# A two-stage kernel on one core: output bursts placed between the next batch's inverse transforms, and four bursts of the first gate kept for a later slot

## The chip, the cores and the metric

The kernel runs on one core of a Trainium2 chip. The metric is the device time of one execution in microseconds. Before the change it is 217.06 us (median of 8 runs, 214.51 to 221.0). The engines named here are TensorE (PE; its weight loads are PEld), VectorE (DVE), ScalarE (ACT), GpSimd (POOL) and SyncE (SP), which only issues DMAs in this kernel.

## What is computed

Attention with eight heads, of which some see all earlier positions and the others only the first four and the last 64; then a gated long convolution over the sequence. For a batch of 4, a sequence of 768, 8 heads of 64, and 512 channels:

```python
scores = scale * np.matmul(q, k.transpose(0, 1, 3, 2))
scores = np.where(mask[None], scores, -1e9)      # causal; and sink or window where not retrieval
a = np.exp(scores - scores.max(-1, keepdims=True))
x = np.matmul(a / a.sum(-1, keepdims=True), v)   # then (batch, seq, 512)

x1, x2, x3 = np.split(x @ w_proj, 3, axis=-1)
X2 = np.fft.rfft(x2, n=S, axis=1)
H = np.fft.rfft(filter_fft, n=S, axis=0)[None]
y = x1 * np.fft.irfft(X2 * H, n=S, axis=1) * x3
out = y @ w_out
```

## The kernel before

**Slots.** The main loop goes over sixteen pairs of heads (n = 0 to 15; four pairs make a batch). One pass, a *slot*, issues for pair n the scores in three thirds of two chunks each (`emit_chunks`, L362, each chunk followed by an exp on ACT into `pT`, L377), a mask multiplication on DVE (`emit_masking`, L384), and for pair n-1 the product with v (`emit_values`, 42 matmuls at L395) and the division (`emit_norm`, L405 and L406). The result `attn` is turned into `xT`, either by PE and a DVE copy (L413, L415) or by a transposing DMA (L417).

**Loads.** Each slot also issues on SP the loads of v (pair n+2) and of q and k (pair n+3), has POOL cast q, k and v to bf16 (L115), and, from pair 6 on, has a transposing DMA make `qkT` for pair n+2 (L147). SP and POOL keep the order in which the kernel's code runs. PE, DVE and ACT keep it until slot 5 (`order.close()` at L595); from there on a scheduler places the instructions when the kernel is built, and every engine then runs its own list in that fixed order.

**Gates.** The second half is a generator, `moe(b, xT)`, here called gate b+1. Whatever it issues between two `yield`s is a *burst*; `gate_step()` in the main loop runs one burst. Slot 4 has three gate steps and every later slot five; a gate that ends hands over to the next. A gate has 21 bursts:

- three that project x2 (eight matmuls at L428, a copy, a sum and a difference, L433 and L434);
- the first projection of x1 (L444, copied at L452), then three forward transforms X (six matmuls at L301, copied at L488), whose nine products with the filter (L479 to L481) are put into a list and taken from it one or two at a time;
- five that alternate between the product g = x1 · x3 (L498, reading the projection of x3 from PSUM) and the next projection of x1;
- three inverse transforms, `convolve(cb, by)`: six matmuls into `c_ps` (L460), a copy of one half on ACT (L463), the sum and the difference on DVE (L465, L466), and the multiplication by g into `y` (L467);
- the fourth channel block in three bursts: projection of x1, `convolve`, and the multiplication by the projected x3 (L510);
- three output bursts: eight matmuls each with `w_out` (L516), a copy to `o_sb` on ACT (L526) and a write of 512 KB from SP (L527).

The fourth gate runs after the attention has ended and has a finer output stage of its own (L531 to L554).

**Buffers.** PSUM is four bank pairs used in turn under one tag (`bank_pair`), by scores, values, turns and gates alike. `y` and `g` have one buffer each, and serve in the set-up under the tags "y" and "g" for `angle`, `size`, `filt` and `fold`. `o_sb` has two.

Of the kernel before, what the change touches and what calls it, by code (L numbers as in the profile page):

```python
# [9 lines left out]
FP32 = mybir.dt.float32  # L10
BF16 = mybir.dt.bfloat16
# [33 lines left out]
def kernel(  # L45
# [13 lines left out]
    nc = tc.nc  # L59

    B, H, S, D = q.shape
    NT = S // 128
    DM = moe_w_proj.shape[0]
    NC = DM // 128
# [4 lines left out]
    HS = S // 2  # L69
    NM = HS // 128  # L70
# [6 lines left out]
    msb = ctx.enter_context(tc.tile_pool(name="moe_sb", bufs=1))  # L77
# [6 lines left out]
    state = {}  # L84
# [18 lines left out]
    BIASED = 4  # L103
# [111 lines left out]
    )  # L215

    turns = msb.tile([128, NM, HS], I32, name="turns", tag="P")
    angle = msb.tile([128, NM, HS], FP32, name="angle", tag="g")
    size = msb.tile([128, NM, HS], FP32, name="size", tag="y")
    for m in range(NM):  # L220
        nc.scalar.activation(out=turns[:, m], in_=fcol, func=AF.Copy, scale=tfrac[:, m:m + 1])
    emit_cast(state[0])
# [73 lines left out]
    def emit_forward(src, tiles, matrix=G):  # L296

        ps = bank_pair("X_ps")
        for u, (t, r) in enumerate(tiles):
            for m in range(NM):  # L300
                nc.tensor.matmul(ps[:, u, :], lhsT=matrix[:, t, m, :], rhs=src[:, r, m, :],  # L301
                                 start=(m == 0), stop=(m == NM - 1))
        return ps
# [4 lines left out]

    def setup_steps():
        filt = state["filt"]  # L310
        fold = msb.tile([128, 2, NM, DM], BF16, name="fold", tag="y")
        nc.vector.tensor_add(fold[:, 0], filt[:, 0:NM, :], filt[:, NM:NT, :])
        nc.vector.tensor_sub(fold[:, 1], filt[:, 0:NM, :], filt[:, NM:NT, :])
        yield

        def put(engine, out, in_, w):
            if engine is nc.scalar:
                engine.activation(out=out, in_=in_, func=AF.Copy, scale=w / S)
            else:
                engine.tensor_scalar(out=out, in0=in_, scalar1=w / S, scalar2=None, op0=ALU.mult)  # L320


        ps = emit_forward(fold, ((0, 0), (1, 0)))
        for out_, in_, w in ((HA[:, 0, 0, :], ps[:, 0], 1), (HA[:, 0, 1, :], ps[:, 0], 0),
                             (HB[:, 0, 0, :], ps[:, 1], 2), (HB[:, 0, 1, :], ps[:, 1], 0)):
            nc.scalar.activation(out=out_, in_=in_, func=AF.Copy, scale=scales[:, w:w + 1])
        put(nc.scalar, HA[0:1, 0, 1, :], ps[0:1, 1], 1.0)
        yield
        ps = emit_forward(fold, ((2, 1), (3, 1)))
        put(nc.vector, HA[:, 1], ps[:, 0, None, :].to_broadcast([128, 2, DM]), 2.0)  # L330
        put(nc.vector, HB[:, 1, 0, :], ps[:, 1], -2.0)
        put(nc.vector, HB[:, 1, 1, :], ps[:, 1], 2.0)
        yield
        put(nc.vector, HA[:, 2], emit_forward(fold, ((4, 0), (5, 1))), 2.0)
        yield
        nc.scalar.activation(out=HB[:, 2], in_=emit_forward(fold, ((6, 0), (7, 1))), func=AF.Copy, scale=scales[:, 3:4])
        yield
# [84 lines left out]
    def moe(b, xT):  # L422
# [11 lines left out]
            nc.vector.tensor_sub(x2[:, 1, m, :], x2s[:, 0], x2s[:, 1])  # L434
            yield
        P = msb.tile([128, 3, 2, DM], BF16, name="P")
        g = msb.tile([128, NC - 1, S], BF16, name="g")
        y = msb.tile([128, NC, S], BF16, name="y")

        def project(part, cb):  # L440
            ps = bank_pair("x13_ps")
            for s in range(2):
                for cc in range(NC):
                    nc.tensor.matmul(ps[:, s, 0:HS],  # L444
                                     lhsT=wproj[:, cc, part * DM + cb * 128:part * DM + (cb + 1) * 128],
                                     rhs=xT[:, cc, s * HS:s * HS + HS],
                                     start=(cc == 0), stop=(cc == NC - 1))
            return ps[:, :, 0:HS]

        def first(cb):  # L450
            x1s = msb2.tile([128, 2, HS], BF16, name="x1s")
            nc.scalar.copy(out=x1s, in_=project(0, cb))  # L452
            return x1s

        def convolve(cb, by):
            ch = slice(cb * 128, (cb + 1) * 128)
            ps = bank_pair("c_ps")
            for r in range(2):
                for n, (tile_no, t, u) in enumerate(((2 * r, r, 0), (2 * r + 1, r, 1), (4 + r, 2, r))):
                    nc.tensor.matmul(ps[:, r, 0:HS], lhsT=P[:, t, u, ch], rhs=Gi[:, tile_no],  # L460
                                     start=(n == 0), stop=(n == 2))
            evs = msb2.tile([128, HS], FP32, name="evs")
            nc.scalar.copy(out=evs, in_=ps[:, 0, 0:HS])  # L463
            conv = msb2.tile([128, S], BF16, name="conv")
            nc.vector.tensor_add(conv[:, 0:HS], evs, ps[:, 1, 0:HS])  # L465
            nc.vector.tensor_sub(conv[:, HS:S], evs, ps[:, 1, 0:HS])  # L466
            nc.vector.tensor_mul(y[:, cb, :], conv, by)  # L467

        products = []

        def multiply(t, X):
            if t == 2:
                swapped = msb.tile([128, 2, DM], BF16, name="swapped")
                nc.sync.dma_start(out=swapped[0:64], in_=X[64:128])
                nc.sync.dma_start(out=swapped[64:128], in_=X[0:64])
            else:
                swapped = X[:, ::-1, :]
            m2 = msb2.tile([128, 2, DM], BF16, name="m2")
            products.append(lambda: nc.vector.tensor_mul(P[:, t], X, HA[:, t]))  # L479
            products.append(lambda: nc.vector.tensor_mul(m2, swapped, HB[:, t]))  # L480
            products.append(lambda: nc.vector.tensor_add(P[:, t], P[:, t], m2))  # L481

        x1s = first(0)
        yield
        for t in range(3):
            X = msb2.tile([128, 2, DM], BF16, name="X", bufs=3)
            ps = emit_forward(x2, ((0, 0), (1, 1)), G2) if t == 2 else emit_forward(x2, ((2 * t, t), (2 * t + 1, t)))
            nc.scalar.copy(out=X, in_=ps)  # L488
            multiply(t, X)
            if t > 0:  # L490
                products.pop(0)()
            yield
        for cb in range(NC - 1):
            if cb > 0:
                x1s = first(cb)
                products.pop(0)()
                yield
            nc.vector.tensor_mul(g[:, cb, :].rearrange("p (s t) -> p s t", s=2), x1s, project(2, cb))  # L498
            for product in range(2 if cb else 1):
                products.pop(0)()  # L500
            yield
        for cb in range(NC - 1):
            convolve(cb, g[:, cb, :])
            yield
        x1s = first(NC - 1)
        yield
        convolve(NC - 1, x1s.rearrange("p s t -> p (s t)"))
        yield
        last_y = y[:, NC - 1, :].rearrange("p (s t) -> p s t", s=2)
        nc.vector.tensor_mul(last_y, last_y, project(2, NC - 1))  # L510
        yield

        def emit_out(ps, i, cbs):
            for cb in cbs:
                for n in range(ps.shape[1]):
                    nc.tensor.matmul(ps[:, n, :], lhsT=y[:, cb, (i + n) * 128:(i + n + 1) * 128],  # L516
                                     rhs=wout[:, cb, :], start=(cb == 0), stop=(cb == NC - 1))
# [18 lines left out]
        for i in range(NT):  # L536
# [15 lines left out]
            else:  # L552
                nc.scalar.copy(out=o_last[:, i], in_=ps[i][:, 0])
            nc.sync.dma_start(out=out[b, i * 128:(i + 1) * 128, :], in_=o_last[:, i])  # L554
        yield


    emit_loads(1)
# [4 lines left out]
    emit_v(state[0])  # L563
    emit_loads(3)

    gates = []

    def gate_step():
        while gates:
            try:  # L570
                next(gates[0])
                return
            except StopIteration:
                gates.pop(0)

    def emit_weights(n):
        if n == 0:
            state["filt"] = filt = msb.tile([128, NT, DM], BF16, name="filt", tag="g")
            nc.gpsimd.dma_start(out=filt, in_=moe_filter_fft.rearrange("(t p) c -> p t c", p=128))
            emit_matrix()  # L580
        for part in {2: (1,), 4: (0, 2)}.get(n, ()):
            cols = slice(part * DM, part * DM + DM)
            nc.gpsimd.dma_start(out=wproj[:, :, cols], in_=moe_w_proj.rearrange("(c p) n -> p c n", p=128)[:, :, cols])
        if n == 7:
            nc.gpsimd.dma_start(out=wout, in_=moe_w_out.rearrange("(c p) n -> p c n", p=128))
# [3 lines left out]
    for n, (b, hp) in enumerate(pairs):  # L589
# [75 lines left out]
            emit_prep(state[n + 2])  # L665
        if hp == 0:
            gates.append(moe(b - 1, last["xT"]))
        gate_step()
        if n <= BY_PE and hp > 0:
            emit_turn(last)  # L670
        emit_chunks(st, 2)
        emit_masking(st, 2)
        if n == 5:
            emit_inverse_matrix()
        gate_step()
    last = state[N - 1]
    emit_values(last)
    emit_norm(last)
# [3 lines left out]
    gates.append(moe(B - 1, xT))  # L682
    while gates:
        gate_step()


# [33 lines left out]
```

## Time and profile before

| what | value |
|---|---|
| median of 8 runs | 217.06 us (214.51 to 221.0) |
| the profiled execution | 214.91 us, its span 213.1 us |
| granted clock of PE, mean over the span | 0.997 |
| DMA moved | 35.27 MB, 166 GB/s over the span |
| scores' exps, L377 (ACT) | 96, 83.2 us |
| projections, L444 (PE) | 256, 45.6 us |
| convolve matmuls, L460 (PE) | 96, 17.7 us |
| output matmuls, L516 (PE) | 92, 21.5 us |
| output copies, L526 (ACT) | 9, 1014 ns each |
| writes of o_sb | 9 of 512 KB, 4.0 us from issue to landing (median) |

The profile is of one execution, and all sums inside it go against 214.91 us. Busy PE is not PE at its peak: matmuls overlap, so what eight of them cost the queue is read from the starts on the timeline (8 of 128x512 in 1.73 to 1.83 us), not from the mean of one.

### The profile page before, as it was taken

The page shows a single profiled execution, that of the slowest core. Times are in us where ns is not written, and L with a number is a line of the kernel's source. Part 1 is how long each engine was busy: PE and PEld are TensorE (multiplying, and loading weights), DVE is VectorE, ACT ScalarE, POOL GpSimd, SP SyncE. Part 2 cuts the span into 40 slices and gives each one's busy share as a digit, 9 for nine tenths or more (in the row PEclk, how much of TensorE's full clock was granted, in tenths as well). Part 3 has the DMA queues.
Part 4 walks back from the last instruction along what each step waited for, and adds up shares of the span by engine and source line. Part 5 has one row for each costly group of instructions (what it writes and reads, how often), then busy time and mean ns, then how long its engine had stood idle before and what let it go on. Part 6 is the DMA issues. An engine that isn't in the chain of part 4 may idle for free.

```text
span 213.1 us, 4337 instructions
## 1 busy us (share of the span) xinstructions
PE 192.2 (90%) x1763; PEld 106.1 (50%) x1763; DVE 153.5 (72%) x254; ACT 147.6 (69%) x183; POOL 68.2 (32%) x110
## 2 busy tenths in 40 slices
PE   7879998898987979989977978999999899999991
PEld 2346766444545554536454535445456464445641
DVE  7847877995799797416798697437796971368970
ACT  7799886996874758568966575797968723772421
POOL 6499366905370164350433351513000000000000
PEclk9999999999999999999999999999999999999998
DMA  5999999998999999969988989992530203402007
GB/s 155 270 305 203 291 268 230 184 213 165 195 200 165 201 230 159 246 249 216 187 177 148 202 136 210 215 264 67 98 78 11 42 0 119 180 0 49 0 36 260
DMA packets 89939, 35.27 MB, mean 166 GB/s; under 512 B 80320, under 2 KB 86464, under 8 KB 89920
## 3 DMA queue, kind: packets, MB, share of 16 engines
q1 hardware_dynamic: 87024, 32.13, 69.3%
q0 software_dynamic: 2896, 2.88, 8.6%
q8 instruction: 13, 0.21, 0.4%
q14 instruction: 6, 0.05, 0.1%
HBM read 24.65 MB, written 6.29 MB: 145 GB/s over the span
## 4 chain that ended last, share of the span: by engine, by line
PE 44%; DVE 28%; DMA 9%; ACT 8%; SPq 3%; issue 3%; POOL 2%; ACTq 0%; DVEq 0%; POOLq 0%
PE x_ps L444 13%; PE x_ps L428 9%; PE out_ps L516 7%; DMA qk_f<-in_k_dram 7%; DVE pT L384 4%; PE att L395 4%; PE X_ps L301 4%; ACT pT L377 4%; DVE m L480 3%; DVE P L479 3%; SPq L95 3%; PE sc L362 3%; PE c_ps L460 3%; DVE conv L465 3%; DVE P L481 3%
## 5 line engine op out<-in xcount | busy, mean ns | idle before, releaser
L377 ACT ACTIVATE pT<-sc 128x1024 bf16<-128x1024 f32 x96 | 83.2, 921 | 18.9 <-PE sc L362 14.4
L444 PE MATMUL x_ps<-xT,wproj 128*128 128x384 bf16 x256 | 45.6, 326 | 5.0 <-DVE conv L466 1.9
L115 POOL CAST qk_bf<-qk_f 128x768 bf16<-128x768 f32 x31 | 27.0, 878 | 68.1 <-DMA qk_f<-in_q_dram 60.0
L384 DVE TENSOR_TENSOR pT<-pT,mask 128x1024 bf16<-128x1024 bf16 x36 | 26.3, 731 | 14.2 <-ACT pT L377 14.1
L444 PEld LDWEIGHTS <-wproj 128*128 128x128 bf16 x256 | 24.2, 98 | 23.3 <-issue 4.8
L362 PE MATMUL sc<-qkT 64*128 64x512 bf16 (+3 forms) x256 | 28.4, 307 | 3.2 <-DVE qkT L143 1.2
L395 PEld LDWEIGHTS <-pT 128*128 128x128 bf16 x672 | 23.2, 97 | 4.2 <-DVE pT L384 1.0
L395 PE MATMUL att<-v_aug,pT 128*128 128x65 bf16 x352 | 24.0, 193 | 1.3 <-DVE pT L384 0.9
L428 PE MATMUL x_ps<-wproj,xT 128*128 128x512 bf16 x96 | 22.4, 379 | 1.3 <-ACT o_sb L526 0.8
L516 PE MATMUL out_ps<-wout,y 128*128 128x512 bf16 x92 | 21.5, 380 | 0.9 <-DVE y L510 0.9
L395 PE MATMUL att<-v_far,pT 128*128 128x65 bf16 x320 | 21.0, 193 | 0.0
L452 ACT CAST x1s<-x_ps 128x768 bf16<-128x768 f32 x16 | 12.9, 806 | 9.7 <-PE x_ps L444 7.1
L362 PEld LDWEIGHTS <-qkT 64*128 64x128 bf16 x256 | 10.0, 94 | 18.8 <-issue 12.4
L460 PE MATMUL c_ps<-Gi,P 128*128 128x384 bf16 x96 | 17.7, 326 | 1.9 <-DVE conv L466 1.1
L347 POOL TENSOR_TENSOR v_far<-v_aug,vmask 128x520 bf16<-128x520 bf16 x16 | 18.5, 1158 | 1.3
L526 ACT COPY o_sb<-out_ps 128x1024 f32<-128x1024 f32 x9 | 9.0, 1014 | 11.7 <-PE out_ps L516 8.9
L301 PE MATMUL X_ps<-x,G 128*128 128x512 bf16 x72 | 16.9, 380 | 0.1
L406 DVE TENSOR_TENSOR attn<-att,rec 128x768 bf16<-128x768 f32 x16 | 15.3, 956 | 0.5
L432 ACT CAST x2s<-x_ps 128x1024 bf16<-128x1024 f32 x12 | 12.4, 1030 | 3.5 <-PE x_ps L428 3.2
L498 DVE TENSOR_TENSOR g<-x1s,x_ps 128x768 bf16<-128x768 bf16 x12 | 11.4, 950 | 4.6 <-PE x_ps L444 4.6
L428 PEld LDWEIGHTS <-xT 128*128 128x128 bf16 x96 | 8.9, 98 | 11.6 <-issue 1.9
L433 DVE TENSOR_TENSOR x<-x2s 128x512 bf16<-128x512 bf16 x12 | 5.1, 424 | 12.9 <-ACT x2s L432 12.8
(94 smaller groups left out, 240.9 us busy)
## 6 DMA issues: line engine op xcount, KB each, us to landing
qk_f<-in_q_dram SPq DMA_DIRECT2D x16, 384.0 KB, 6.5
qk_f<-in_k_dram SPq DMA_DIRECT2D x16, 384.0 KB, 6.8
v_f<-in_v_dram SPq DMA_DIRECT2D x16, 384.0 KB, 5.4
out_dram<-o_sb SPq DMA_DIRECT2D x9, 512.0 KB, 4.0
wproj<-in_moe_w_proj_dram POOLq DMA_DIRECT2D x3, 512.0 KB, 9.3
out_dram<-o_last SPq DMA_DIRECT2D x5, 256.0 KB, 2.5
swapped<-X SPq DMA_DIRECT2D x8, 128.0 KB, 2.3
filt<-in_moe_filter_fft_dram POOLq DMA_DIRECT2D x1, 768.0 KB, 10.8
```

What stands on the lines that cost most here:

```text
L115: nc.gpsimd.tensor_copy(out=out, in_=in_)
L301: nc.tensor.matmul(ps[:, u, :], lhsT=matrix[:, t, m, :], rhs=src[:, r, m, :], start=(m == 0), stop=(m == NM - 1))
L347: nc.gpsimd.tensor_mul(v_far, v_aug[:, 0:4], vmask[:, hp, :, :, None].to_broadcast([128, 4, 2, 65]))
L362: nc.tensor.matmul(sc[:, hh, n * 128:(n + cnt) * 128], lhsT=qkT[rows, 1, j * 128:(j + 1) * 128], rhs=qkT[rows, 0, i * 128:(i + cnt) * 128] ...
L377: nc.scalar.activation(out=pT[:, :, c, 0:w], in_=sc[:, :, 0:w], func=AF.Exp, scale=SCALE)
L384: nc.vector.tensor_mul(near, near, which)
L395: nc.tensor.matmul(att[:, hh, 65 * i:65 * i + 65], lhsT=st["pT"][:, hh, c, 128 * n:128 * n + 128], rhs=st["v_far" if i >= j + 2 else "v_au ...
L406: nc.vector.tensor_mul(st["attn"].rearrange("p i hh d -> p hh i d"), rows[:, :, :, 0:64], rec[:, :, :, None].to_broadcast([128, 2, NT, 64]))
L428: nc.tensor.matmul(ps[:, half, :], lhsT=xT[:, cc, half * HS + m * 128:half * HS + (m + 1) * 128], rhs=wproj[:, cc, DM:2 * DM], start=(cc = ...
L444: nc.tensor.matmul(ps[:, s, 0:HS], lhsT=wproj[:, cc, part * DM + cb * 128:part * DM + (cb + 1) * 128], rhs=xT[:, cc, s * HS:s * HS + HS], ...
L460: nc.tensor.matmul(ps[:, r, 0:HS], lhsT=P[:, t, u, ch], rhs=Gi[:, tile_no], start=(n == 0), stop=(n == 2))
L516: nc.tensor.matmul(ps[:, n, :], lhsT=y[:, cb, (i + n) * 128:(i + n + 1) * 128], rhs=wout[:, cb, :], start=(cb == 0), stop=(cb == NC - 1))
```

## The change

It does three things.

1. **Outputs move into the next gate.** The output bursts become a generator of their own, `output(b, y)`, which a gate leaves in the list `outputs` when it has finished `y`. The next gate takes it, and runs one of its bursts after each of its first three `convolve` bursts; the loop now goes over all four channel blocks. The fourth gate's own outputs run at the very end.
2. **y has two buffers and g none.** The product x1 · x3 is written into `y` itself (`second`), and `convolve` multiplies it in place. The set-up tiles `angle`, `size`, `filt` and `fold` all use the tag "y", in turn.
3. **Fewer gate steps in slots 5 to 7.** The last gate step of a slot is left out before slot 8, and in slot 7 another one. The first gate has 18 bursts now, of which four remain for slot 8. All nine products are taken from the list before the last `second`.

```diff
-        g = msb.tile([128, NC - 1, S], BF16, name="g")
-        y = msb.tile([128, NC, S], BF16, name="y")
+        y = msb.tile([128, NC, S], BF16, name="y", bufs=2)
...
+        def multiply_next(count):
+            for product in range(count):
+                products.pop(0)()
...
-        for cb in range(NC - 1):
-            if cb > 0:
+        def second(cb, x1s):
+            nc.vector.tensor_mul(y[:, cb, :].rearrange("p (s t) -> p s t", s=2), x1s, project(2, cb))
+
+        second(0, x1s)
+        multiply_next(2)
+        yield
+        x1s = first(1)
+        multiply_next(2)
+        yield
+        second(1, x1s)
+        multiply_next(2)
+        yield
+        x1s = first(2)
+        multiply_next(1)
+        yield
+        second(2, x1s)
+        yield
+        earlier = outputs.pop(0) if outputs else iter(())
+        for cb in range(NC):
+            if cb == NC - 1:
                 x1s = first(cb)
-                products.pop(0)()
                 yield
-            nc.vector.tensor_mul(g[:, cb, :].rearrange("p (s t) -> p s t", s=2), x1s, project(2, cb))
-            for product in range(2 if cb else 1):
-                products.pop(0)()
+            convolve(cb, y[:, cb, :] if cb < NC - 1 else x1s.rearrange("p s t -> p (s t)"))
             yield
-        for cb in range(NC - 1):
-            convolve(cb, g[:, cb, :])
-            yield
-        x1s = first(NC - 1)
-        yield
-        convolve(NC - 1, x1s.rearrange("p s t -> p (s t)"))
-        yield
+            for step in earlier:
+                yield
+                break
         last_y = y[:, NC - 1, :].rearrange("p (s t) -> p s t", s=2)
         nc.vector.tensor_mul(last_y, last_y, project(2, NC - 1))
         yield
-
+        outputs.append(output(b, y))
+
+    def output(b, y):
...
-        gate_step()
+        if n != 2 * BIASED - 1:
+            gate_step()
         if n <= BY_PE and hp > 0:
             emit_turn(last)
         emit_chunks(st, 2)
         emit_masking(st, 2)
         if n == 5:
             emit_inverse_matrix()
-        gate_step()
+        if n >= 2 * BIASED:
+            gate_step()
...
     while gates:
         gate_step()
+    for step in outputs.pop():
+        pass
```

More of the change, by code (lines that the diff above doesn't have):

```diff
@@ L217 @@
     turns = msb.tile([128, NM, HS], I32, name="turns", tag="P")
-    angle = msb.tile([128, NM, HS], FP32, name="angle", tag="g")
-    size = msb.tile([128, NM, HS], FP32, name="size", tag="y")
+    angle = msb.tile([128, NM, HS], FP32, name="angle", tag="y", bufs=2)
+    size = msb.tile([128, NM, HS], FP32, name="size", tag="y", bufs=2)
     for m in range(NM):
@@ L310, in setup_steps @@
         filt = state["filt"]
-        fold = msb.tile([128, 2, NM, DM], BF16, name="fold", tag="y")
+        fold = msb.tile([128, 2, NM, DM], BF16, name="fold", tag="y", bufs=2)
         nc.vector.tensor_add(fold[:, 0], filt[:, 0:NM, :], filt[:, NM:NT, :])
@@ L490, in moe @@
             if t > 0:
-                products.pop(0)()
+                multiply_next(1)
             yield
-        for cb in range(NC - 1):
-            if cb > 0:
+        def second(cb, x1s):
[10 more added lines that the diff above has]
+        x1s = first(2)
+        multiply_next(1)
+        yield
[4 more added lines that the diff above has]
+            if cb == NC - 1:
                 x1s = first(cb)
-                products.pop(0)()
                 yield
-            nc.vector.tensor_mul(g[:, cb, :].rearrange("p (s t) -> p s t", s=2), x1s, project(2, cb))
-            for product in range(2 if cb else 1):
-                products.pop(0)()
+            convolve(cb, y[:, cb, :] if cb < NC - 1 else x1s.rearrange("p s t -> p (s t)"))
             yield
-        for cb in range(NC - 1):
-            convolve(cb, g[:, cb, :])
-            yield
-        x1s = first(NC - 1)
-        yield
-        convolve(NC - 1, x1s.rearrange("p s t -> p (s t)"))
-        yield
+            for step in earlier:
+                yield
+                break
         last_y = y[:, NC - 1, :].rearrange("p (s t) -> p s t", s=2)
@@ L554, in moe @@
             nc.sync.dma_start(out=out[b, i * 128:(i + 1) * 128, :], in_=o_last[:, i])
-        yield
     emit_loads(1)
@@ L564 @@
     emit_loads(3)
-    gates = []
+    gates, outputs = [], []
     def gate_step():
@@ L577, in emit_weights @@
         if n == 0:
-            state["filt"] = filt = msb.tile([128, NT, DM], BF16, name="filt", tag="g")
+            state["filt"] = filt = msb.tile([128, NT, DM], BF16, name="filt", tag="y", bufs=2)
             nc.gpsimd.dma_start(out=filt, in_=moe_filter_fft.rearrange("(t p) c -> p t c", p=128))
```

## The prediction

> **What bounds the kernel now.** I read the page's first two parts, then the table by stretches of time, then the waits of TensorE (PE), and last the timeline around each wait.[...]
>
> ```profile
> PE 192.2 (90%) x1763; PEld 106.1 (50%) x1763; DVE 153.5 (72%) x254; ACT 147.6 (69%) x183; POOL 68.2 (32%) x110
> PEclk9999999999999999999999999999999999999998
> 60.00:75.00 15.00, 13.01 (x133) 7.73 (x132) 13.03 (x20) 9.62 (x14) 4.26 (x5) 1.00 1.08 191
> 105.00:120.00 15.00, 12.58 (x117) 7.18 (x115) 12.94 (x17) 10.14 (x13) 7.12 (x9) 1.00 0.88 169
> 120.00:135.00 15.00, 12.79 (x148) 7.43 (x147) 12.68 (x21) 9.62 (x14) 4.13 (x6) 1.00 1.08 189
> 135.00:150.00 15.00, 15.00 (x125) 7.27 (x123) 6.84 (x14) 12.29 (x15) 5.23 (x8) 1.00 0.69 176
> 174.00:190.00 16.00, 16.00 (x82) 7.58 (x81) 6.33 (x13) 8.60 (x9) 0.00 (x0) 1.00 0.27 99
> 190.00:205.40 15.40, 15.23 (x92) 8.67 (x90) 14.04 (x24) 5.33 (x8) 0.00 (x0) 1.00 0.08 17
> ```
>
> The columns of the stretches are length, then PE, weight load, VectorE (DVE), ScalarE (ACT) and GpSimd (POOL) busy, each with its instructions, then granted clock, DMA share, GB/s. PE is the bound overall, at full clock. But it alternates. In 135–150 (the outputs and the first bursts of a gate) PE is full and DVE works 6.84 of 15 us. In 105–135 (products, projections and inverse transforms of gate 2) DVE works 25.6 of 30 us and PE loses 4.6. Gate 1 has the same dip in 60–75. The last 31 us, where no attention is left, are dense on PE already.
>
> ```profile
> PE x_ps L444 <- DVE conv L466: 1.9, 2, 1.1
> PE x_ps L444 <- DVE g L498: 1.7, 2, 1.0
> PE c_ps L460 <- DVE conv L466: 1.1, 1, 1.1
> PE att L395 <- DVE pT L384: 0.9, 1, 0.9
> PE out_ps L516 <- DVE y L510: 0.9, 2, 0.7
> PE x_ps L428 <- ACT o_sb L526: 0.8, 1, 0.8
> PE c_ps L460 <- ACT x1s L452: 0.4, 1, 0.4
> ACT o_sb L526 <- DMA out_dram<-o_sb: 2.9, 1, 2.9
> ```
>
> (Total us, times, longest.) Nearly all of PE's waits after 58 us are for DVE, and most of those in the convolve stage: a convolve burst costs PE six matmuls, 0.98 us, but DVE 0.46 + 0.46 + 0.47 = 1.4 us (starts of L465, L466, L467 on the timeline), and a pair of PSUM banks is given back only by L466. Between 58 and 175 us the PE gaps over 0.12 us add up to 9.8 us; that is all the change can win, for its PE instructions are the same in number.
>
> **The change part by part.**
>
> *Outputs between the next gate's convolve bursts.* The three output bursts of a batch (each 8 matmuls of 0.216 us, 1.73 us of PE, one 1.01 us ACT copy, one 512 KB write, nothing on DVE) leave the end of their own gate and stand after the first three convolve bursts of the next one. The instruction order of both builds shows it: before, PE has `c_ps` 12, attention, `c_ps` 6, projection, `c_ps` 6 in gate 2; after, `c_ps` 6, attention, `out_ps` 8, `c_ps` 6, `out_ps` 8, `c_ps` 6, `out_ps` 8. DVE's 1.4 us per convolve is now covered by 1.73 us of PE work that asks nothing of it. The waits of that stage in gates 2 and 3 go: 1.07 (at 122.40) + 0.45 (126.35) + 0.71 (131.67, an output waiting for its own y) + 0.79 (168.49) = **3.0 us**. If the cover were gone (an output late for its bank pair), what is next in line is that same 1.4 us a burst.
>
> *Output copies apart.* At 90 us ACT's third o_sb copy waits for the first one's write to land (o_sb has two buffers, the write took 5.2 us), and its PSUM pair holds PE for 0.80. After, first to third output are 0.98 + 0.54 + 1.73 + 0.43 + 0.98 + 1.73 = 6.4 us of PE work apart: **0.8 us** gone. In the tail they are 0.98 + 1.73 + 0.98 + 1.73 = 5.4 us apart, against a median landing of 4.0 there: nothing lost.
>
> *Gate 1 thinned.* It has no earlier outputs, and now gets 4, 4 and 3 bursts in slots 5, 6 and 7 where it got 5 each; four (two convolves, a projection, the last multiply) stay for slot 8, the ninth. Its waits were 0.33 + 0.54 + 0.38 + 0.73 + 0.35 (products) + 1.10 (convolve). The gate's share of DVE per slot falls by a fifth to two fifths there. From none to all of 3.4 could go; I take half of the 1.10 and a third of the rest, **1.35 us**. What is late next there is the attention chain itself (scores, exp, mask, values), with less filler between; that is part of the loss below.
>
> *Products of gate 2, one slot's share.* Its first burst falls into slot 8 and two into slot 9, so slot 10 loses the last L498 (0.86) and gains X's third burst. Two products move ahead: slot 10 has 2 x 0.86 + 8 x 0.60 = 6.5 us of them on DVE where it had 3 x 0.86 + 7 x 0.60 = 6.8. Taken as nothing; the 2.3 us of waits there (109.03, 111.57, 115.59) stay, between gone and doubled. [...] The row first: the four products beside POOL's casts of 103.9–108.7 took 1.31, 1.19, 1.30 and 1.53 us where the median is 0.69, so 2.6 us lost, 0.65 each, and the waits follow right behind. [...]
>
> *In place of g.* L498 writes y, L467 multiplies in place; same engine, shapes and counts: nothing. The set-up tiles share y's two buffers in turn, each behind the tile it was behind before: nothing. Second y buffer: only frees.
>
> *Queues.* POOL's order is the same. On SP the three writes of batch 0 leave the place where they held the queue 6.67 us (87.26) ahead of a transposing load of qkT, and come three slots or so later, ahead of those for pairs 13 and 14. Those landed at 130.7 and 142.2 and were used at 140.35 and 151: over 8 us of slack against a delay of the same 6.7. Hidden; if not, PE's scores wait the difference. ACT has three copies of 1.01 us between exps; it is busy 9.6 of 15 us there: hidden.
>
> *The tail.* Gate 4 now carries batch 2's outputs. PE was dense before (16.00 of 16, 15.23 of 15.4), so filling gains nothing. 24 output matmuls (5.2 us) more come after the attention's end and as many fewer before it: zero as long as the attention ends 5.2 us plus the gain earlier. The final y still has 1.3 + 1.95 us of PE work beside it (projection and nine output matmuls) against 0.2 + 0.5 + 0.46 + 0.46 + 0.56 + 0.95 = 3.1 us of ACT and DVE: 0 to 0.5 lost.
>
> *New waits.* Every seam is new; gates 2 to 4 now begin with PE-heavy and end with mixed bursts, and slot 7 has the least filler. The trace cannot show it. Bounds: none, and one 0.5 us wait in each of the eleven slots, 5.5. The nearest row is the seam of slots 13 to 15, where the old mix gave 0.28 + 0.79 in three slots; I take **1.2 us**.
>
> *Sum:* 3.0 + 0.8 + 1.35 - 1.2 = 3.95 us of the profiled execution's 214.91 (span 213.1), 1.84%. That execution is near the lowest of the eight; scaled to the median 217.06 it gives 213.1.
>
> **The rivals.**
>
> *A: as summed.* 2.5 to 5.5 us gained, 211.5 to 214.5. For it: DVE's idle is in the wrong place, 6.84 against 12.9 in 15.
>
> *B: the waits re-form.* DVE's order is a queue; masks and norms of the next pair stand behind convolves in new places, or POOL's casts hit the product phase harder. Then 0 to 2 us are gained: 215 to 217, likeliest 216. For it: every wait of 109–117 is for DVE in its products, which the change hardly thins. Against: the convolve stage has 4.1 of the 9.8 us, and there the cover is new.
>
> *C: the loads set the pace (slower).* Place: slot 8's first scores, which need the transposed qkT of pair 8. SP issued it at 70.82 behind loads in a saturated stretch (share 1.08), it landed 5.2 us later, at 76.0, and was used at 81.99. After, 28 matmuls fewer stand ahead of that use, 4.6 us: 77.4. Slack 1.4 us. From 5.35 us of lateness (1.4 + 3.95) it decides: slower. One such transfer took 12.3 us (issued 40.80); a repeat lands at 83.1, 5.7 us of waiting, 1.8 us lost, 218.9. And as 5.2 us of output work has left that stretch, PE has nothing to put there. Against it: nine of the ten landed in 3.7 to 6.4 us, and what was ahead of the slow one (the first loads of the program) is over by then.
>
> *D: it does not do what it says.* Excluded for the order (PE's stream is fixed and shows the outputs between); what can fail is only the effect, which is B.
>
> **How the numbers follow.** A 0.66, B 0.23, C 0.11. About 1% is what a measurement of this kernel can tell from no change, so faster means under 214.9, slower over 219.2. A gives 0.61 faster and 0.05 within; B 0.04 faster, 0.18 within, 0.01 slower; C 0.05 within and 0.06 slower. Faster 0.65, same 0.28, slower 0.07. The range 210.7 to 217.0 has A with its full bounds (up to 6.4 us won: all the convolve waits, all of gate 1's) and B; outside are C and a small rest of A.
>
> **What would show it.** Right: in the waits of PE the lines with L466 and L510 all but gone, also ACT's o_sb waiting for its write; DVE's busy time in the stretches of gate 2 evener, PE's over 14 of 15; the values of pair 8 start about 6 us earlier; the stretch after the last attention about 5 us longer and still dense. B: the same waits under L498's new form (y), L384 or L406. C: scores of pair 8 waiting for the DMA of qkT. Wrong: a PE sum that grows (the clock under 1.00, matmuls slower), or waits of over 2 us in the tail.

## The result, and the profile after

| | before | after |
|---|---|---|
| median, measured side by side | 216.60 us (32 runs, 213.80 to 223.09) | 213.41 us (11 runs, 211.47 to 216.58) |
| ratio after to before | | 0.9867 [0.9829, 0.9906] |
| the profiled execution, and its span | 214.91, 213.1 us | 213.41, 211.7 us |
| PE idle in gaps over 0.12 us, from slot 5's values to 175 us | 9.82 us | 8.28 us |
| granted clock over the span | 0.997 | 0.990 |

The change makes the kernel 1.3% faster, some 2.9 us; a second measurement of the same kernel, among the experiments, gave 0.9906 [0.9856, 0.9957], 2.0 us. Here and below a ratio and its interval use only executions within 1.5% of the fastest of the same kernel, while a median uses all, so the two can differ. The two profiles differ by less, 1.5 us, because the profiled execution of before is one of the five fastest of its 32. And not all of the 1.5 us lies in the changed part: 1.2 of it is there before any moved burst runs: the matmuls with v of slot 5 (slot 5's values, below) start at 53.1 us before and at 52.0 after, and in the fourteen profiles of this study at anything from 52.0 to 59.6. From there to the end of PE's work it is 155.65 us before and 155.08 after, 0.6 less. So the profiles are read here for where PE waits, and the medians for how much it is worth.

The page of after: busy time of the engines, and PE's granted clock by slice.

```profile
PE 192.6 (91%) x1763; PEld 106.4 (50%) x1763; DVE 157.4 (74%) x254; ACT 147.8 (70%) x183; POOL 70.9 (33%) x110
PEclk9999999999979999999999999999999999999999
```

Busy times are those of before within 4 us; what is new is a 7 in the clock of slice 12, near 60 us. The waits of PE between 90 and 175 us (gates 2 and 3), total, times and longest:

```profile
PE x_ps L444 <- DVE y L498: 2.4, 2, 1.6
PE X_ps L301 <- DVE attn L406: 1.0, 1, 1.0
PE x_ps L444 <- DVE attn L406: 0.3, 1, 0.3
PE out_ps L533 <- ACT pT L377: 0.2, 1, 0.2
```

No line with L466 or with the gate's last multiplication (L510, now L525) is left in these gates, and ACT's o_sb copy no longer waits for its write. What is left waits for `second`, the old L498 in its new form, or for the values' normalisation L406. The stretches (length, then PE, PEld, DVE, ACT and POOL busy with their instructions, clock, DMA share, GB/s):

```profile
103.00:118.00 15.00, 13.11 (x153) 7.81 (x152) 13.42 (x22) 9.87 (x13) 4.53 (x6) 1.00 1.02 177
118.00:133.00 15.00, 15.00 (x134) 7.78 (x133) 11.51 (x19) 12.92 (x18) 4.49 (x6) 1.00 1.06 208
133.00:148.00 15.00, 14.96 (x154) 7.97 (x153) 12.15 (x19) 13.03 (x16) 6.04 (x8) 1.00 0.67 129
168.00:184.00 16.00, 16.00 (x84) 8.09 (x83) 8.66 (x18) 8.85 (x11) 0.00 (x0) 1.00 0.18 67
184.00:204.00 20.00, 19.92 (x112) 10.68 (x110) 13.66 (x22) 7.77 (x11) 0.00 (x0) 1.00 0.27 92
```

Before, DVE had 12.68 us of work in one 15 us stretch and 6.84 in the next; now it has 11.51 and 12.15 (second and third row), and PE is full in both. The products of gate 2 in the first row gain little: PE works 13.11 of 15 us there, 12.58 before. The last two rows are the tail with the three more outputs in it: still dense.

And a new hole. The timeline around 58 us, slot 5 of the changed kernel (start, duration, engine, line, operation; in brackets the idle time before it and who ended it; other rows of the stretch are left out):

```profile
56.94 1.30 DVE L483 TENSOR_TENSOR P<-X,HAB 128x1024 bf16<-128x1024 bf16 x1
57.69 1.24 POOL L115 CAST v_aug<-v_f 128x768 bf16<-128x768 f32 x1
58.17 1.30 DVE L484 TENSOR_TENSOR m<-X,HAB 128x1024 bf16<-128x1024 bf16 x1
59.01 1.37 POOL L347 TENSOR_TENSOR v_far<-v_aug,vmask 128x520 bf16<-128x520 bf16 x1
59.40 0.55 DVE L415 COPY xT<-xt_ps 128x768 bf16<-128x768 bf16 x1
59.99 0.39 PE L362 MATMUL sc<-qkT 64*128 64x256 bf16 x4 [1.93 <-DVE xT L415]
```

Scores of the next pair need a PSUM pair. It is held by the turn of the last pair until DVE's copy L415 has emptied it, and that copy stands in DVE's queue behind two products, 1.30 us each beside POOL's casts. Before, PE had a projection burst (L444, eight matmuls) at this place, and 0.54 us of the wait were left behind it:

```profile
58.84 1.46 PE L444 MATMUL x_ps<-xT,wproj 128*128 128x384 bf16 x8 [0.33 <-ACT X L488]
60.84 0.61 PE L362 MATMUL sc<-qkT 64*128 64x512 bf16 x6 [0.54 <-DVE xT L415]
```

The gate step left out of slot 5 took that burst from ahead of these scores. PE then runs at about half clock, as the rows for the wait and for what follows it show:

```profile
57.00:60.70 3.70, 1.44 (x15) 0.61 (x12) 3.70 (x5) 3.23 (x5) 3.62 (x5) 1.00 0.64 135
60.70:64.20 3.50, 3.50 (x13) 1.69 (x12) 2.90 (x5) 0.75 (x1) 0.42 (x1) 0.51 0.92 114
```

PE was busy for 1.44 of 3.70 us, and then its clock was at 0.50 for 3.41 us (60.74 to 64.15), in which it had work throughout: about 1.7 us of work lost. Sixteen projection matmuls take 4.46 us there; before, sixteen took 2.77 at a clock of 1.00.

### The profile page after: what moved, and what is told of

The parts are those of the page before. It is cut to its first block, busy times and chain, and to the rows that moved or that the text cites. A ratio compares the mean times of both kernels' runs of the same rounds, so it can differ in the third digit from the quotient of the medians.

```text
span 211.7 us, 4337 instructions
## 1 busy us (share of the span) xinstructions
PE 192.6 (91%) x1763; PEld 106.4 (50%) x1763; DVE 157.4 (74%) x254; ACT 147.8 (70%) x183; POOL 70.9 (33%) x110
## 4 chain that ended last, share of the span: by engine, by line
PE 57%; DVE 22%; ACT 10%; DMA 3%; issue 3%; POOL 3%; SPq 1%; ACTq 0%; DVEq 0%; POOLq 0%
PE x_ps L444 16%; PE out_ps L533 9%; PE x_ps L428 8%; PE c_ps L460 7%; PE att L395 6%; ACT pT L377 5%; PE sc L362 4%; PE X_ps L301 4%; DVE pT L384 3%; DMA qk_f<-in_k_dram 3%; DVE attn L406 3%; DVE P L483 3%; DVE qkT L143 2%; DVE m L484 2%; ACT X L492 2%
## 5 line engine op out<-in xcount | busy, mean ns | idle before, releaser
L444 PE MATMUL x_ps<-xT,wproj 128*128 128x384 bf16 x256 | 47.3, 335 | 3.6 <-DVE y L498 2.4
L115 POOL CAST qk_bf<-qk_f 128x768 bf16<-128x768 f32 x31 | 28.0, 910 | 64.8 <-DMA qk_f<-in_q_dram 58.7
L384 DVE TENSOR_TENSOR pT<-pT,mask 128x1024 bf16<-128x1024 bf16 x36 | 27.8, 771 | 12.6 <-ACT pT L377 12.3
L444 PEld LDWEIGHTS <-wproj 128*128 128x128 bf16 x256 | 24.8, 100 | 23.5 <-issue 7.8
L460 PE MATMUL c_ps<-Gi,P 128*128 128x384 bf16 x96 | 18.3, 326 | 0.1
L115 POOL CAST v_aug<-v_f 128x768 bf16<-128x768 f32 x16 | 15.4, 965 | 3.3 <-DMA v_f<-in_v_dram 3.3
L406 DVE TENSOR_TENSOR attn<-att,rec 128x768 bf16<-128x768 f32 x16 | 15.3, 956 | 0.5
L465 DVE TENSOR_TENSOR conv<-evs,c_ps 128x384 bf16<-128x384 f32 x16 | 8.8, 550 | 9.1 <-ACT evs L463 9.1
L301 PEld LDWEIGHTS <-G 128*128 128x128 bf16 x96 | 8.8, 98 | 11.7 <-DVE attn L406 1.3
```

The costliest lines, as they stand in the source:

```text
L115: nc.gpsimd.tensor_copy(out=out, in_=in_)
L384: nc.vector.tensor_mul(near, near, which)
L406: nc.vector.tensor_mul(st["attn"].rearrange("p i hh d -> p hh i d"), rows[:, :, :, 0:64], rec[:, :, :, None].to_broadcast([128, 2, NT, 64]))
L444: nc.tensor.matmul(ps[:, s, 0:HS], lhsT=wproj[:, cc, part * DM + cb * 128:part * DM + (cb + 1) * 128], rhs=xT[:, cc, s * HS:s * HS + HS], ...
```

## The experiments

Ratios are to the kernel before on the same chip, with 95% intervals. An interval covers the executions of one measurement; two measurements of one kernel can lie further apart, as the turn on ACT will show (0.980 and 0.994). Edits are diffs on the changed kernel unless said otherwise. The theory at the start: the outputs between the convolves bring the gain, the thinning of gate 1 costs. The rivals: the thinning brings it (DVE relieved in slots 5 to 7); or neither, and what counts is only that y is doubled or that the outputs come later.

**Outputs alone (e1_outputs_only).** All gate steps are kept.

```diff
-        if n != 2 * BIASED - 1:
-            gate_step()
+        gate_step()
...
-        if n >= 2 * BIASED:
-            gate_step()
+        gate_step()
```

> The changed kernel with all five gate steps kept in slots 5 to 7, so only the outputs are moved (and y has two buffers). Theory (outputs between the convolves carry the gain, thinning gate 1 carries none, because in the profile it opened a wait of 1.93 us in slot 5 and lowered the clock): ratio to the kernel before 0.980 to 0.988, at least as fast as the changed kernel, and no PE wait over 1 us near 58 us. Rival (thinning carries a third of the gain, as the prediction had it with 1.35 of 3.95 us): 0.987 to 0.993.

0.9894 [0.9844, 0.9945], 215.31 us. The waits of gates 2 and 3 for the convolves are gone but for 0.28 us, and the ratio lies between the two measured for the whole change. The wait for xT at 60 us is 1.28 us here instead of 1.93, but the profile has a half-clock stretch too, elsewhere:

```profile
84.40:87.70 3.30, 1.39 (x15) 0.66 (x13) 3.18 (x5) 1.77 (x3) 2.05 (x2) 1.00 1.16 241
87.70:91.10 3.40, 3.40 (x12) 0.97 (x11) 0.22 (x1) 1.03 (x2) 0.82 (x1) 0.51 1.36 208
```

**Thinning alone (e2_thin_only).** The same edit the other way, on the kernel before.

```diff
-        gate_step()
+        if n != 2 * BIASED - 1:
+            gate_step()
...
-        gate_step()
+        if n >= 2 * BIASED:
+            gate_step()
```

> The kernel before with only the gate steps of slots 5 to 7 reduced to 4, 4 and 3; the outputs stay at the end of their own gate. Theory (thinning alone gives nothing): ratio 0.996 to 1.010, with the wait for the copy of xT at 58 us as in the changed kernel and the convolve waits of gates 2 and 3 still there. Rival (thinning is worth 1.35 us by itself): 0.990 to 0.996.

1.0026 [0.9982, 1.0069], 218.12 us: no gain. Its waits of PE from 58 to 175 us:

```profile
PE sc L362 <- DVE xT L415: 2.4, 1, 2.4
...
PE x_ps L444 <- DVE conv L466: 1.1, 1, 1.1
PE c_ps L460 <- DVE conv L466: 1.0, 2, 0.6
PE out_ps L516 <- DVE y L510: 0.8, 1, 0.8
```

The wait for xT comes with the thinning, without any moved output; the convolve waits stay as long as the outputs do. The mean clock of this profile is 0.989, beside 0.990 in that of the changed kernel.

**y in place alone (e3_inplace_only).** The two y buffers and the new order of the products are kept; outputs go back to their own gate, with all gate steps.

```diff
-        earlier = outputs.pop(0) if outputs else iter(())
+        earlier = iter(())
...
-        outputs.append(output(b, y))
+        if b < B - 1:
+            yield from output(b, y)
+        else:
+            outputs.append(output(b, y))
```

> The kernel before with only the form of the gate changed: y with two buffers in place of g, products in place, the nine products taken as in the changed kernel; outputs at the end of their own gate, five gate steps in every slot. Theory (this carries nothing): ratio to the kernel before 0.995 to 1.005. Rival (the second y buffer or the earlier products are what helps): 0.985 to 0.993.

0.9951 [0.9901, 1.0001], 216.25 us. That is not told apart from no change, and up to 1% is not excluded either. The waits of the convolve stage are still there (1.06, 0.31, 0.78 and 0.79 us, in a profiled execution of 222.78 us).

**Outputs in the next gate, but together (e6_delayed_together).** They run after the gate's last multiplication; everything else is as in the changed kernel.

```diff
-            for step in earlier:
-                yield
-                break
         last_y = y[:, NC - 1, :].rearrange("p (s t) -> p s t", s=2)
         nc.vector.tensor_mul(last_y, last_y, project(2, NC - 1))
         yield
+        yield from earlier
```

> The changed kernel with the three outputs of the earlier batch still in the next gate, but together after its last multiplication and not between its convolves. Theory (the gain comes from standing between the convolves): the waits for L466 and y in the convolve stage of gate 2 are back (over 1.5 us there), ratio 0.996 to 1.010. Rival (the gain comes from delaying output work out of the stretch in which the loads come in, or from filling the end of the next gate): 0.983 to 0.992.

0.9976 [0.9910, 1.0043], 217.83 us: the gain is gone. The waits of PE between 90 and 175 us:

```profile
PE x_ps L444 <- DVE y L498: 3.1, 2, 2.3
PE out_ps L531 <- DVE y L522: 1.3, 1, 1.3
...
PE c_ps L460 <- DVE conv L466: 0.8, 1, 0.8
PE x_ps L444 <- DVE conv L466: 0.8, 1, 0.8
```

So neither the later time of the outputs nor the second y brings it, but their place between the convolves. Part of this kernel's loss is of another kind: its profile has a mean clock of 0.980 and two half-clock stretches, one with sixteen projection matmuls in 4.19 us (62.04), one with two output matmuls in 0.81 (130.90). From slot 5's values to the end of PE's work it takes 159.17 us; without the two, at 1.7 us each, that would be about 155.8 (an estimate), as before the change (155.65). The ratio rests on three of twelve executions, so the waits are the better evidence here.

**One step back into slot 5 (e4_fill_slot6).** It puts the projection burst back ahead of the scores that waited for xT.

```diff
-        if n >= 2 * BIASED:
+        if n == 5 or n >= 2 * BIASED:
```

> The changed kernel with the last gate step of slot 5 put back, so that one projection of eight matmuls stands ahead of the scores that wait for the copy of xT. Theory (the missing filler makes the wait of 1.93 us, and this wait makes the clock fall to 0.76 in 58 to 65 us, 1.7 us lost): wait at most 0.6 us, granted clock of that stretch 1.00, 1.5 to 3 us faster than the changed kernel. Rival (the slow clock has another cause): the wait goes, the clock of that stretch stays under 0.9, at most 1.4 us faster.

0.9899 [0.9841, 0.9957], 215.79 us. The wait fell from 1.93 to 0.52 us and the profile's clock is 1.00 throughout, as expected, but the time did not follow. Other waits came back: in gate 1 0.65 and 0.34 us for L498, 0.66 and 0.38 for exps and 0.33 for the division, and in gate 2 the three of before (0.90, 0.44, 0.96). From slot 5's values to the end of PE's work it takes 155.06 us, against 155.08 in the changed kernel with its half-clock stretch. The expected gain of a filled hole did not come; the burst covers one wait and, by shifting the seams, opens others.

**The turn's copy on ACT (e5_turn_on_act, e14_turn_again).** For pair 4 alone, so that the bank is freed without DVE's queue.

```diff
-            nc.vector.tensor_copy(out=st["xT"][:, st["pair"][1], :], in_=ps)
+            (nc.scalar.copy if st["n"] == 4 else nc.vector.tensor_copy)(out=st["xT"][:, st["pair"][1], :], in_=ps)
```

> The changed kernel with one instruction moved: the copy of xT of pair 4 goes from DVE, where it stands behind two products slowed by POOL, to ACT. Theory (the place of that copy on DVE makes the wait, the wait the slow clock): the wait of 1.93 us falls under 1 us, clock 1.00 there, 1 to 3 us faster than the changed kernel. Rival (pace of the loads: qkT of pair 8 landed at 76.7 and was used at about 77): what is won at 58 us is lost at 77 us in a wait of scores for the transposing DMA, same time as the changed kernel within 0.7 us.

> The changed kernel with the copy of xT of pair 4 on ACT, a second time on another chip, because its first ratio (0.9797) and those of the changed kernel (0.9867 and 0.9906) have intervals that touch. Theory (one wait of 1.9 to 2.7 us shrunk to 0.3 is worth 1 to 2 us of time): 0.976 to 0.985. Rival (the slow clock only moves to another stretch and takes it back): 0.985 to 0.992.

First 0.9797 [0.9743, 0.9852], 213.31 us, then, the same kernel on another chip, 0.9937 [0.9891, 0.9984], 214.63 us. Those two intervals do not meet, so a gain over the changed kernel is not shown. What is shown is the mechanism of the wait: 1.93 us became two waits of 0.31 and 0.53. But the half clock did not go: 11 of the 19 executions of this kernel have a mean clock under 0.995, and in the first profile the stretch moved to 78 us:

```profile
74.70:78.10 3.40, 2.04 (x16) 0.73 (x15) 3.33 (x7) 3.40 (x6) 3.01 (x4) 1.00 1.16 236
78.10:81.60 3.50, 3.49 (x12) 1.66 (x12) 2.70 (x5) 1.88 (x3) 0.82 (x1) 0.51 1.95 222
```

**POOL's work on v left out (e9_no_v_on_pool).** Pairs 8 to 15 use the values of pair 7; loads and orders stay. It leaves out the casts of v and the masked v, POOL's work beside the products of gates 2 and 3.

```diff
     def emit_v(st):
+        if st["n"] >= 8:
+            st["v_aug"], st["v_far"] = state[7]["v_aug"], state[7]["v_far"]
+            return
```

> The changed kernel without POOL's casts of v and without the masked copy of v for pairs 8 to 15 (the values of pair 7 are used in their place); every engine's order and all DMAs are the same. Theory (products of gate 2 beside POOL are slow, and PE waits behind them): products 0.69 us each in gate 2 unless beside a cast of q or k, the waits at 96 us (0.97) and 106 us (1.61) both under 0.7, 1 to 2.5 us faster than the changed kernel. Rival (the DVE queue there is late for its own load): products faster, waits of PE as before within 0.5 us, at most 0.7 us faster.

0.9778 [0.9730, 0.9825], 211.19 us, about 1% below the changed kernel (0.9867 and 0.9906). First the changed kernel at the products of gate 2, DVE and POOL:

```profile
99.91 0.97 DVE L483 TENSOR_TENSOR P<-X,HAB 128x1024 bf16<-128x1024 bf16 x1 [2.01 <-ACT X L492]
100.80 1.30 DVE L484 TENSOR_TENSOR m<-X,HAB 128x1024 bf16<-128x1024 bf16 x1
102.14 1.42 DVE L485 TENSOR_TENSOR P<-P,m 128x1024 bf16<-128x1024 bf16 x1
...
100.32 1.24 POOL L115 CAST v_aug<-v_f 128x768 bf16<-128x768 f32 x1
101.64 1.37 POOL L347 TENSOR_TENSOR v_far<-v_aug,vmask 128x520 bf16<-128x520 bf16 x1
```

Then the same three with v left out (lines three further down in that kernel), and the one cast that POOL still has there:

```profile
99.62 0.69 DVE L486 TENSOR_TENSOR P<-X,HAB 128x1024 bf16<-128x1024 bf16 x1 [1.54 <-ACT X L495]
100.23 1.31 DVE L487 TENSOR_TENSOR m<-X,HAB 128x1024 bf16<-128x1024 bf16 x1
101.57 0.69 DVE L488 TENSOR_TENSOR P<-P,m 128x1024 bf16<-128x1024 bf16 x1
...
99.92 1.07 POOL L115 CAST qk_bf<-qk_f 128x768 bf16<-128x768 f32 x1 [0.18 <-DMA qk_f<-in_k_dram]
```

Of these six products, the four that start while a POOL instruction runs (the first of all inside a cast of q or k, 99.51 to 100.34) take 0.97 to 1.42 us, the two that do not 0.69. The timeline of the changed kernel shows eleven two-input 128x1024 instructions of DVE (products and masks) starting inside a cast or masking of v, and five inside a cast of q or k. Fifteen of the sixteen, with 0.23 to 0.98 us of the POOL instruction left, take what is left, less 0.14 or 0.15 us, longer than 0.69; the one with 0.11 left takes 0.68. The one at 100.80 has 100.32 + 1.24 - 100.80 = 0.76 us of the cast ahead of it and takes 1.30 - 0.69 = 0.61 us longer; the one at 102.14 has 0.87 and takes 0.73 longer; here, the one at 100.23 has 0.76 and takes 0.62 longer. PE's wait for `second` at 106 us fell from 1.61 to 0.74 us, and the one of 0.96 at 96 us went. The waits of PE between 90 and 175 us:

```profile
PE x_ps L447 <- DVE y L501: 1.6, 2, 0.8
...
```

POOL's work is on the path here, but not all of the gain need come from it. From slot 5's values to the end of PE's work this profile takes 150.65 us where the changed kernel takes 155.08, and of those 4.4 us 2.4 are waits of PE and 1.7 the half-clock stretch, which this profile does not have (2 of its 6 executions have a clock under 0.995). How far the clearer clock comes from the edit is not shown.

**Products earlier, and the turn on ACT (e10_early_and_act).** The other reading of the wait at 106 us was that too many products stand ahead of `second`.

```diff
-            if t > 0:
-                multiply_next(1)
+            multiply_next((0, 2, 3)[t])
...
-        multiply_next(2)
+        multiply_next(1)
...
-        multiply_next(2)
+        multiply_next(1)
...
-        multiply_next(1)
```

(with the edit of the turn's copy above)

> The changed kernel with the copy of xT of pair 4 on ACT, as in the run that moved only that, and with products taken earlier: two beside the second forward transform and three beside the third, fewer beside the projections. Theory (DVE's queue in the product slot is what is left): the wait of 1.61 us for L498 falls under 1 us, ratio to the kernel before 0.970 to 0.980. Rival (what limits is POOL beside the products, wherever they stand): the wait moves to another instruction, ratio 0.979 to 0.987.

0.9840 [0.9792, 0.9889], 213.02 us, and PE's longest wait for `second` is still 1.60 us. The order of the products did not move it; leaving out POOL's work did.

**Masked v on DVE (e11_far_on_dve), and that with the turn on ACT (e12_far_and_turn).** If POOL beside the products is what costs, its larger instruction there could go to DVE.

```diff
-        nc.gpsimd.tensor_mul(v_far, v_aug[:, 0:4], vmask[:, hp, :, :, None].to_broadcast([128, 4, 2, 65]))
+        if st["n"] < 8:
+            nc.gpsimd.tensor_mul(v_far, v_aug[:, 0:4], vmask[:, hp, :, :, None].to_broadcast([128, 4, 2, 65]))
+
+    def emit_far(st):
+        nc.vector.tensor_mul(st["v_far"], st["v_aug"][:, 0:4],
+                             vmask[:, st["pair"][1], :, :, None].to_broadcast([128, 4, 2, 65]))
...
+        if n >= 8:
+            emit_far(st)
```

> The changed kernel with the masked copy of v of pairs 8 to 15 (v_far) made by DVE one slot later and not by POOL. [...] Rival (DVE is full in the product slots, so any work added there is on the path): 0.3 to 1 us slower.

> The same with the copy of xT of pair 4 on ACT too. Theory (the two waits are apart, and add): ratio to the kernel before 0.970 to 0.980, the fastest complete kernel of the study. Rival (the loads or the new place of v_far take back what is won): not faster than the changed kernel by more than 0.5 us.

0.9963 [0.9925, 1.0002], 217.40 us, and 1.0046 [1.0006, 1.0086], 216.98 us: the gain of the change is lost. The instruction takes 0.69 us on DVE against 1.05 to 1.37 on POOL, but it needs POOL's cast of v first. The first line is a wait of DVE in the former kernel, the second one of PE in the latter:

```profile
DVE v_far L351 <- POOL v_aug L115: 4.0, 3, 1.7
```

```profile
PE sc L367 <- DVE attn L411: 3.6, 1, 3.6
```

DVE's whole queue stands behind `v_far` while it waits for the cast of v. That cast in turn stands in POOL's queue behind those of q and k, which wait for their loads (4.82 us ahead of the one at 90.03 in the former kernel). What is late then (L411, the normalisation that L406 was) holds PE for 3.65 us.

**The changed kernel again (e13_changed_again).** It ran unedited, on the same chip as the two kernels with the masked v on DVE.

> The changed kernel itself, so that the two others of this call stand beside it on the same chip. Both theories: ratio to the kernel before 0.983 to 0.990; about two executions in three with a granted clock of 0.99, that is one or two stretches of half clock, if the thinned slots 5 to 7 make them.

0.9906 [0.9856, 0.9957], 214.80 us. The same waits again: 2.67 us for xT, 1.48 for `second`, and a half-clock stretch. From slot 5's values to the end of PE's work this profile takes 154.49 us. Of the kernels run here that compute everything, none beats the changed one by more than the repeats differ.

## The prediction, step by step

The mechanism was right, and the size somewhat too large: 3.95 us were forecast (1.84%), 2.0 to 2.9 measured (0.9 to 1.3%). That the median of 213.41 lies so near the forecast 213.1 is in part luck: beside it the kernel before took 216.60, not the 217.06 it was scaled to, and the repeat took 214.80. By the gaps of PE from slot 5 on:

| term | predicted, us gained | in the two profiles |
|---|---|---|
| convolve waits of gates 2 and 3 | 3.0 | 2.8 (3.01 before, 0.22 left) |
| o_sb copy behind its write | 0.8 | 0.8 |
| gate 1 thinned | 1.35 | -0.96 (3.43 before, 4.39 after) |
| products of gate 2 and new waits | -1.2 | -1.1 (gate 2 from 2.31 to 2.85, gate 3's products from 0.28 to 0.83) |
| half-clock stretch | not foreseen | -1.7 |

The last column sums to -0.2, where the profiles differ by +0.6 in the changed part; the remaining 0.8 us is spread over gaps and seams too small for this list and is not attributed.

*Outputs between the convolves.* Right in place and size. It is shown by four kernels: with the outputs alone the waits go and the time with them; thinned alone, with y alone, and with the outputs late but together, the waits stay and no clear gain is left. Single ratios lie too close to rank these kernels. But the seven measurements with the outputs between the convolves and POOL's work as it was have 0.980 to 0.994, and the three without outputs there 0.995 to 1.003; no one of either kind reaches into the other, though they come close. One sentence of the prediction says too much: that most of PE's waits after 58 us lie in the convolve stage. By its own later count they are 4.1 of 9.8 us.

*Output copies apart.* The wait is gone as predicted. It was not tried on its own.

*Gate 1 thinned.* This is the step that failed, a term that came out with the wrong sign: "I take half of the 1.10 and a third of the rest, **1.35 us**." The waits of the convolve and the products did shrink. But the bursts left out were also filler, and one of them had covered DVE's queue ahead of a PSUM bank: 1.93 us now lie open, 2.67 in another execution, 2.40 with the thinning alone. "What is late next" was named as the attention chain, and a wait of 0.86 us for an exp is there at 78 us; but the copy of the turn was not looked at. Thinning alone measured 1.0026, so the whole term is worth about nothing where 1.35 us, 0.6%, were counted. That is most of the miss. What the thinning does depends on what it stands with: alone it lengthened gate 1's gaps from 3.43 to 4.98 us, but with the outputs moved they are 5.60 without it and 4.39 with it. And of the executions with a clock of 0.995 or more, the five of the changed kernel have a median of 212.43 us, the three with the outputs alone 214.21. So it may win in gate 1 what it loses by the clock; so few executions do not show it.

*Products of gate 2.* "Taken as nothing" was too kind: the waits grew by 0.54 us, within the bounds given, and leaving out POOL's work on v takes 1.8 us from the two waits of gate 2. The prediction set a row beside it, 0.65 us a product. In size the row was fair: the three products above lost 0.97 + 1.30 + 1.42 - 3 x 0.69 = 1.62 us, 0.54 each. What was left of the running POOL instruction at their starts was 0.43, 0.76 and 0.87 us; at the starts of the row's four, in the profile of before, it was 0.65 to 0.98, and they lost 0.50 to 0.84.

*Queues.* Right, but only just for rival C: the transposing load of pair 8 was issued at 69.86 us, landed at 76.7, and its first scores ran at 77.0. Slack 0.3 us where 1.4 was forecast; no score waited for a DMA.

*The tail.* Right: three outputs more, 5.2 us, and PE dense. The values of pair 8 start at 93.1 us where they started at 99.0, 5.9 us earlier against a forecast of 6 (1.2 of it lies before slot 5, so the size is partly luck), and attention's last values at 162.8 instead of 170.6.

*New waits.* -1.2 was close to the -1.1 of the gaps, in part by luck: half of that stands in the product stage of gate 2, for which nothing was taken. What no step had is the clock; it stood only among the signs of being wrong ("the clock under 1.00"), and that sign appeared in part. Executions with a mean granted clock under 0.995 (the two profiles of the changed kernel, with one half-clock stretch each behind the set-up, have 0.990 and 0.992) are 27 of 86 of the kernel before, and 19 of 24 of the changed kernel. In its 24 executions, the 5 without have a median of 212.43 us, the 19 with 214.47. With 1.7 us a stretch, a share of 0.79 instead of 0.31 is worth 0.8 us on average. It overlaps with the term of gate 1, since with the thinning alone 8 of 12 executions are under 0.995 too, and it stays an estimate: the kernel with a step put back had a clean clock in 4 of its 6 executions and was no faster. How to be rid of the stretch in this kernel is open.

*The rivals.* B (the waits re-form) has a part in it: what is left in gates 2 and 3 are, but for 0.2 us, the waits under L498's new form and L406. A carried the result.

## What to carry to other kernels

Where an engine that is not the bound has its work in lumps, put work that does not need it between the lumps, and look for the gain in the waits of that one stage; the same work moved to the end of the stage gained nothing. Before taking filler out of a slot, ask of each wait behind it what it covered: here a bank that another engine frees from far back in its queue. And compare two profiles for causes, many runs for sizes, and repeat the measurement itself: one kernel measured twice gave 0.980 and 0.994.

## What the hardware showed beyond that

In the changed kernel TensorE's granted clock was 1.00 from 57.33 to 60.74 us, with PE busy for 1.15 of the 3.41 us, then 0.50 from 60.74 to 64.15 with PE busy throughout, then 1.00 again. Ahead of the half clock in the two other stretches shown above it was busy for 1.39 of 3.30 us with the outputs alone and for 2.04 of 3.40 with the turn on ACT.

Sixteen projection matmuls (L444; L447 in the kernel with v left out) follow the wait for xT in four profiles, and their time shows the clock:

| profile | wait for xT, us | the sixteen matmuls, us |
|---|---|---|
| changed kernel | 1.93 | 4.46 |
| changed kernel again | 2.67 | 4.45 |
| outputs together | 1.89 | 4.19 |
| v left out | 1.77 | 2.77 |

So a wait of nearly the same length was followed by half clock in one kernel and not in another. What sets off the half clock is not shown, nor why one kernel has the stretch in some executions and not in others. Where it came it fell on dense work, and there it cost 1.7 us (4.46 less 2.77).

And DVE's products and masks ended late beside POOL by what was left of the running POOL instruction, less 0.14 or 0.15 us: in the changed kernel by 0.09 us where 0.23 was left (51.33 us) and by 0.84 where 0.98 was left (122.54), both masks. A mask that started at 47.48, 0.04 us ahead of two casts that took 2.10, took 0.69. Why the two engines meet like this is not shown.
